# Key blocks on partitions 0 to 95, no zero rows in the value buffers, and an order of tasks from fixed ranks

## The chip, the cores and the metric

The kernel runs on one core of a Trainium2 chip. The core has five engines with instruction streams of their own: TensorE (PE in the profile, with its weight loads as PEld), VectorE (DVE), ScalarE (ACT), GpSimd (POOL) and SyncE (SP), and DMA queues that the engines issue to. The metric is the device time of one execution in microseconds (us). The time before is the median of three runs, 277.43 us (277.42 to 278.05). Every duration below is from one profiled execution, whose span is 275.7 us (275.66 from the first to the last instruction).

## The reference, cut to what matters

B = 4 batches, H = 8 heads, S = 768 positions, D = 64 per head. Attention in chunks of 32 queries over 8 memory keys and a window of 16 keys to the left and 8 to the right; then a Fourier mix over positions and the 512 model channels, a layer norm, and an MLP of 512 to 2048 to 512 with both residuals.

```python
for c in range(S // 32):
    l_start, r_end = max(0, 32 * c - 16), min(S, 32 * c + 32 + 8)
    k_full = np.concatenate([mem_k, k[:, :, l_start:r_end]], axis=2)
    v_full = np.concatenate([mem_v, v[:, :, l_start:r_end]], axis=2)
    a = softmax(q[:, :, 32 * c:32 * c + 32] @ k_full^T / sqrt(D))
    out[:, :, 32 * c:32 * c + 32] = a @ v_full
...
x = out.transpose(0, 2, 1, 3).reshape(B, S, H * D)
mixed = np.real(np.fft.fft(np.fft.fft(x, axis=1), axis=2))
u = x + mixed
un = (u - mean(u)) / np.sqrt(var(u) + 1e-06)
result = u + np.maximum(un @ w_ch1, 0.0) @ w_ch2
```

## The kernel before

**Attention.** There are 16 steps n, each one pair of heads of one batch. q and k are brought in by POOL's DMA queue (`e_load_qk`, L381), turned by TensorE (`e_turn_q`, `e_turn_k`, L409) and copied out of its banks (qT on ScalarE, L427; kTb by L452; the memory keys' columns by L440). v is brought in by SP (`e_load_v`) into one of four buffers `va`, [128, 2, 12, 66] in float32. A tile of such a buffer belongs to 64 queries and has one key per partition: 8 memory keys, 16 of left context, 64 own and 8 of right context, 96 in all. `MEM0` is the partition of the first one, 32 before the change, so the keys stand on partitions 32 to 127; partitions 0 to 31 of `va` are filled with zeros by four copies on ScalarE (`e_low_rows`, L363), and the matching columns of the two `kTb` buffers by a memset. Column D of `va` holds ones, so the value product also gives the softmax's sum. Small memsets and selects (`e_edges` L347 to 349, `e_edge_ones` L354 to 359, `e_masks` L333 to 339) take out keys past the ends.

For each step and each half g of its 12 tiles: 12 score matmuls (`e_scores`, L465), two exponentials (`e_exp`, L475), 24 value matmuls (`e_values`, L517) and the division (`e_norm`, L527 and L528). There is one bank set for scores. Steps 6 to 11 take the form of `a_scores` (L488, L500), and there the PE task `values(n)` of steps 4 to 9 also issues the turns of step n + 2.

**Fourier.** Tables of sines are made at the start: POOL's `e_iota` (L327), angles on VectorE (L342 to L1050), ScalarE's sine for table S (L1188, L1189) and for table D (L1191, L1192), then negatives on VectorE (L1196 to L1202). A one-element activation loads ScalarE's sine functions (L993), another (L1209) its exponential. The first batch (`first_fourier`) folds (L659, L670), splits each value into a high and a low float16 (`hi` on ScalarE, `lo` on VectorE L715), multiplies by the S table (`g_row` L735, `g_rows` L748) and then by the D table (`e_columns`, L759). Batches 1 to 3 do likewise (L549 to L606, rows at L589), the last two with `h_columns` (L780) and `h_mix` (L800, L801); sums with x are at L808 on VectorE or L820 on POOL. Layer norm: statistics on VectorE (`e_stats`, L832 and L833), scale factors on POOL (`e_scale`, L858 to L861), the scaling on ScalarE (L846).

**MLP.** Each batch is three thirds j of 256 rows. The first layer is eight tasks of eight matmuls (`e_ch1`, L897) with a relu on ScalarE (L906). The second layer is plain for batch 0 and (1, 0) (`e_ch2`, L915). For the other eight thirds it is done in seven products of half size: sums of relu blocks on VectorE (`e_s`, L952, in two groups: hidden blocks 0 to 5 and 6 to 7, and one sum more of all eight), products on TensorE (`e_prod`, L964; in the order m1, m2 on the first six blocks, m1, m2 on the last two, m5, m6, m3, m7, m4), and adds to the residual on VectorE (`e_add`, L969) that free the product's bank.

**The order.** Nothing above is emitted in the order of the source. Each piece is a task of class `Plan` with an engine, a cost in us, the tasks it comes after, the buffers it takes and gives back, and a rank. `order()` goes through time, and on each engine starts the task of lowest rank that is ready by its model; the result is the order of instructions on each engine, and the semaphores between engines follow from the data. Where TensorE has nothing near the start, `order()` puts in an idle matmul (`e_fill`, L1024; 20 of them). `shortest(24, 1.5)` calls `order()` 24 times, with normal draws of spread 1.5 added to the ranks, and takes the order that ends first by the model. The tasks' ranks otherwise are the numbers in the `add` calls or the place in the source.

## Time and profile before

| | us |
|---|---|
| median of three runs | 277.43 (277.42 to 278.05) |
| profiled execution, span | 275.66 |
| time outside that span, up to the median | 1.77 |
| TensorE busy | 258.7 (94%) |
| VectorE busy | 204.9 (74%) |
| ScalarE busy | 160.6 (58%) |
| POOL busy | 78.5 (28%) |

The profile's page gives the busy time of each engine, then the span in 40 slices with the busy share in tenths (a 9 is 90% or more), then the chain of work that ended last. A line of the chain has a start, a length, an engine, the operation and the tile, and the line of the kernel. The timeline lists instructions or runs of like instructions: start, length from the first start to the last end, engine, line, operation, out<-in, shape and count, and in brackets the idle time before and what ended it. A window line has the stretch, its length, and then the busy time and number of instructions of PE, PEld, DVE, ACT and POOL, the granted clock, the DMA share and GB/s.

### The profile page before, as it was taken

Reading aid. Unit: us, or ns where it says so; the run is one execution under the profiler, and the core shown is the slowest. Engines: PE = TensorE matmul, PEld = TensorE weight load, DVE = VectorE, ACT = ScalarE, POOL = GpSimd, SP = SyncE. Lnnn points to the kernel's source line nnn. Section 1 sums busy time; section 2 is a strip of 40 time slices with the busy share of each in tenths; the row PEclk is TensorE's granted clock in tenths of the full one; section 3 lists DMA queues with packets and bytes.
Section 4 is the critical chain, followed back from the end, with each engine's and each line's share of the span. In section 5 each row is a group of like instructions: output and inputs, shape, how many; then the busy total and the mean of one; then the engine's idle time right before and its main releaser. Section 6 shows DMA issues by size and latency. Waiting matters only on the chain.

```text
span 275.7 us, 8160 instructions
## 1 busy us (share of the span) xinstructions
PE 258.7 (94%) x3365; PEld 209.8 (76%) x3365; DVE 204.9 (74%) x460; ACT 160.6 (58%) x300; POOL 78.5 (28%) x146
## 2 busy tenths in 40 slices
PE   0489999999999999999999989999999998999995
PEld 0367797888756788658669868888889887888884
DVE  7978999840337999998995997839997996354444
ACT  6888647888555688277646627555373483615150
POOL 8852652350111054045046246001100371000000
PEclk9999999999999999999999999999999999999999
DMA  6999999999997979958989964644960424313152
GB/s 104 203 176 176 193 211 205 198 195 200 174 190 176 204 170 175 212 79 160 241 144 199 183 118 117 123 117 146 132 182 1 95 62 83 111 40 76 64 90 76
DMA packets 116118, 39.98 MB, mean 145 GB/s; under 512 B 104561, under 2 KB 111473, under 8 KB 116081
## 3 DMA queue, kind: packets, MB, share of 16 engines
q1 hardware_dynamic: 93888, 23.54, 47.4%
q0 software_dynamic: 21472, 15.21, 34.8%
q10 hardware_dynamic: 720, 0.72, 0.8%
q8 instruction: 26, 0.43, 0.7%
q14 instruction: 12, 0.09, 0.1%
HBM read 37.36 MB, written 13.37 MB: 184 GB/s over the span
## 4 chain that ended last, share of the span: by engine, by line
PE 80%; DVE 11%; POOL 4%; ACT 2%; issue 1%; POOLq 0%; DVEq 0%
PE ph L897 26%; PE pc L964 14%; PE pc L915 10%; PE ps L589 6%; PE xa L517 5%; PE xo L517 4%; PE pm L759 3%; PE ps L748 3%; DVE S L952 2%; PE sc L465 2%; DVE st L832 2%; DVE xsb L969 2%; PE trk L409 2%; PE idle L1024 1%; PE trq L409 1%; DVE hT L952 1%
## 5 line engine op out<-in xcount | busy, mean ns | idle before, releaser
L897 PE MATMUL ph<-unT,w_sb 128*128 128x256 f16 x768 | 89.6, 273 | 0.0
L897 PEld LDWEIGHTS <-w_sb 128*128 128x128 f16 x768 | 73.7, 98 | 9.3 <-issue 0.3
L906 ACT ACTIVATE hT<-ph 128x512 f16<-128x512 f32 x96 | 56.3, 600 | 39.9 <-PE ph L897 21.1
L964 PEld LDWEIGHTS <-hT 128*128 128x128 f16 x320 | 30.8, 98 | 7.1 <-issue 2.0
L964 PE MATMUL pc<-w_sb,hT 128*128 128x256 f16 x256 | 32.1, 273 | 1.3 <-DVE xsb L969 0.9
L969 DVE TENSOR_TENSOR xsb<-pc,xsb 128x256 f32<-128x256 f32 x57 | 23.7, 420 | 12.6 <-PE pc L964 10.8
L915 PE MATMUL pc<-w_sb,hT 128*128 128x512 f16 x128 | 29.8, 380 | 0.0
L500 ACT ACTIVATE e<-sc,mbias 128x192 f32<-128x192 f32 (+1 forms) x48 | 19.2, 489 | 8.8 <-PE sc L488 8.8
L915 PEld LDWEIGHTS <-hT 128*128 128x128 f16 x128 | 11.8, 98 | 12.9 <-issue 0.4
L952 DVE TENSOR_TENSOR S<-hT 128x768 f16<-128x768 f16 (+1 forms) x16 | 8.5, 533 | 16.1 <-ACT hT L906 15.7
L475 ACT ACTIVATE e<-sc,mbias 128x384 f32<-128x384 f32 x32 | 17.0, 575 | 4.6 <-PE sc L465 4.3
L846 ACT ACTIVATE un<-xsb,rs 128x512 f16<-128x512 f32 x16 | 12.4, 810 | 9.8 <-POOL rs L861 9.8
L964 PE MATMUL pc<-w_t,S 128*128 128x256 f16 x128 | 16.0, 273 | 1.3 <-DVE xsb L969 1.1
L832 DVE BATCH_NORM_STATS2 st<-xsb 128x6 f32<-128x512 f32 x24 | 16.3, 680 | 0.3
L820 POOL TENSOR_TENSOR xsb<-mix,xr 128x512 f32<-128x512 f32 x6 | 8.7, 1459 | 26.6 <-ACT mix L814 26.6
L517 PEld LDWEIGHTS xa<-va,e 128*64 128x64 f32 x384 | 12.9, 142 | 3.8 <-issue 2.7
L601 ACT CAST up<-ps 128x386 f16<-128x386 f32 x16 | 9.7, 606 | 10.4 <-PE ps L589 9.4
L964 PEld LDWEIGHTS <-S 128*128 128x128 f16 x128 | 12.3, 98 | 3.7 <-issue 1.6
L517 PE MATMUL xa<-va,e 128*64 128x65 f32 x384 | 15.2, 230 | 0.0
L517 PE MATMUL xo<-va,e 128*64 128x65 f32 x384 | 14.1, 223 | 0.0
L574 ACT CAST hi<-ff 128x768 f16<-128x768 f32 x12 | 9.7, 829 | 6.3 <-DVE ff L566 6.1
L517 PEld LDWEIGHTS xo<-va,e 128*64 128x64 f32 x384 | 12.6, 138 | 0.5 <-ACT ff L683 0.3
(189 smaller groups left out, 471.9 us busy)
## 6 DMA issues: line engine op xcount, KB each, us to landing
va<-in_v_dram SPq DMA_DIRECT2D x32, 220.0 KB
w_sb<-in_moe_w_ch_dram POOLq DMA_DIRECT2D x8, 512.0 KB, 15.7
out_dram<-xsb SPq DMA_DIRECT2D x12, 256.0 KB
qs<-in_q_dram POOLq DMA_DIRECT2D x12, 192.0 KB, 6.4
ks<-in_k_dram POOLq DMA_DIRECT2D x12, 192.0 KB, 6.9
x_rows<-xsb POOLq DMA_DIRECT2D x3, 768.0 KB, 4.5
xr<-x_back POOLq DMA_DIRECT2D x3, 768.0 KB, 6.0
out_rows<-xsb SPq DMA_DIRECT2D x9, 256.0 KB
```

The source lines that it names most:

```text
L475: nc.scalar.activation(e1[:, :, :, ts(half, 32)], sc[:, :, 0:6, ts(half, 32)], AFT.Exp, bias=mbias[:, half:half + 1], scale=1.0 / math.sqr ...
L500: nc.scalar.activation(to, src, AFT.Exp, bias=mbias[:, half:half + 1], scale=1.0 / math.sqrt(D))
L517: nc.tensor.matmul(xa[64 * half:64 * half + 64, st, hh, 0:65], e1[:, hh, t6, :], v1[:, hh, 6 * g + t6, 0:65], start=True, stop=True)
L589: nc.tensor.matmul(out_[:, sp, :], part[:, ab, sp * 3 + st, c0:c1], tab[:, sp, st, :], start=(st == 0 and i == 0), stop=(st == 2 and i == 1))
L832: nc.vector.bn_stats(st6, xs[b][:, kt, :])
L846: nc.scalar.activation(un, xs[b][:, kt, :], AFT.Identity, bias=rs[:, 1:2], scale=rs[:, 0:1])
L897: nc.tensor.matmul(ph[:, k, :], w1_sb[:, dt, ts(HH * k + i, P)], unT_of[b, j][:, dt, :], start=(dt == 0), stop=(dt == NDT - 1))
L906: nc.scalar.activation(hT_of[b, j][:, :, i, :], ph, AFT.Relu, bias=0.0, scale=1.0 if (b, j) in FAST else -1.0)
L915: nc.tensor.matmul(pc_of[b, j, r], hT_of[b, j][:, k, i, ts(r, P)], w2_sb[:, HH * k + i, :], start=(i + k == 0), stop=(i + k == HH))
L952: nc.vector.tensor_tensor(out_[:, lo:hi], a[:, lo:hi], c[:, lo:hi], op)
L964: nc.tensor.matmul(pc_of[key], a[:, i, :], w[:, i, :], start=(i == 0 and new), stop=(i == HH - 1), skip_group_check=not new)
L969: nc.vector.tensor_tensor(u, pc, u, ALU.add)
```

## The change

The first key goes from partition 32 to partition 0 (`MEM0 = 0`), and `KEYS` = 96 is the number of partitions that are used. The masks and edges move along; `kTb` is set to zero in columns 96 to 127 instead of 0 to 31; the exponential writes 96 partitions instead of 128; a value product contracts over 96 rows instead of 128. The zero fill of `va` and its four tasks go.

`shortest` is replaced by `settled`, which gives 92 tasks (by their number) a fixed rank and calls `order()` once. Tasks in `after` that were not there before are added at several places (folds and splits of the first batch, rows, columns, sums, products, stores); they order tasks in the plan and emit nothing. The order of instructions of every engine changes with this. As built, these moves bear on the text below:

- ScalarE: the two zero copies ahead of the sines and the two among the exponentials are gone. The first exponential stands ahead of the D sines, and the program has four function-table loads on ScalarE, where it had two: for the S sines, the first exponential, the D sines, the next exponential.
- POOL: `e_iota` stands behind the q and k loads of steps 0 and 1 and one `kTb` memset; it was first. VectorE takes the memory keys' casts ahead of the angles, and the first kT copy (L452) ahead of the last two folds of the D angles.
- SP: the v load of step 1 is first and that of step 0 second; the loads from step 6 on, the output stores and the flips change places.
- TensorE: 18 idle matmuls instead of 20; turns and scores of steps 4 and 5 go ahead of some of the first batch's rows and columns; `h_columns(2, 2)`, `rows` of batch 3 and `h_columns(3, 2)` stand between m6 and m3 of the thirds (1, 1), (2, 0) and (2, 2).
- VectorE: in those thirds the statistics or the fold, which stood ahead of sums or adds, come behind them; POOL's L820 tasks move with the new order of the sums, and one of them, with tasks of scale factors, stands at the sums of the third (1, 2).

```diff
 BIGM = 800.0
-MEM0 = 32
+MEM0 = 0
 OWN = MEM0 + NMEM + LEFT
+KEYS = OWN + 2 * CHUNK + RIGHT
...
 
-    def shortest(self, tries, spread):
-
...
-            placed = self.order()
-            if found is None or self.end < found[0]:
-                found = (self.end, i)
-        return placed
+    def settled(self, moved):
+
+        for no, rank in moved.items():
+            self.tasks[no]["rank"] = rank
+        return self.order()
...
         nc.gpsimd.memset(mbias, 0.0)
-        nc.gpsimd.memset(mbias[96:128, 0:1], NEG)
+        nc.gpsimd.memset(mbias[64:96, 0:1], NEG)
         nc.gpsimd.affine_select(out=mbias[:, 1:2], in_=mbias[:, 1:2], compare_op=ALU.is_ge,
                                 fill=NEG, base=-(OWN - LEFT + CHUNK), pattern=[[0, 1]],
                                 channel_multiplier=1)
-        nc.gpsimd.memset(mbias[0:MEM0, 1:2], 0.0)
...
         eng.memset(v1[:, :, :, D:D + 1], 1.0)
-        eng.memset(v1[32:64, :, 0, 0:D], 0.0)
-        eng.memset(v1[96:128, :, NT - 1, 0:D], 0.0)
+        eng.memset(v1[0:32, :, 0, 0:D], 0.0)
+        eng.memset(v1[64:96, :, NT - 1, 0:D], 0.0)
 
     def e_edge_ones(i):
         v1 = va[i]
-        lo, hi = v1[32:64, :, 0, D:D + 1], v1[96:128, :, NT - 1, D:D + 1]
-        nc.gpsimd.affine_select(out=lo, in_=lo, compare_op=ALU.is_ge, fill=0.0, base=32 - OWN,
+        lo, hi = v1[0:32, :, 0, D:D + 1], v1[64:96, :, NT - 1, D:D + 1]
+        nc.gpsimd.affine_select(out=lo, in_=lo, compare_op=ALU.is_ge, fill=0.0, base=-OWN,
                                 pattern=[[0, 2], [0, 1]], channel_multiplier=1)
         nc.gpsimd.affine_select(out=hi, in_=hi, compare_op=ALU.is_ge, fill=0.0,
-                                base=OWN + 63 - 96, pattern=[[0, 2], [0, 1]],
+                                base=OWN + 63 - 64, pattern=[[0, 2], [0, 1]],
                                 channel_multiplier=-1)
         nc.gpsimd.memset(v1[MEM0:MEM0 + NMEM, :, 0, D:D + 1], 1.0)
-
-    def e_low_rows(i):
-        low = va[i][0:MEM0].rearrange("p h t c -> p (h t c)")
-        nc.scalar.copy(low, zero[0:MEM0].to_broadcast([MEM0, 2 * NT * 66]))
...
         for half in halves:
-            nc.scalar.activation(e1[:, :, :, ts(half, 32)], sc[:, :, 0:6, ts(half, 32)],
-                                 AFT.Exp, bias=mbias[:, half:half + 1],
+            nc.scalar.activation(e1[0:KEYS, :, :, ts(half, 32)], sc[0:KEYS, :, 0:6, ts(half, 32)],
+                                 AFT.Exp, bias=mbias[0:KEYS, half:half + 1],
...
         for half in range(2) if g else (part,):
-            to, src = (e1[:, part, :, ts(half, 32)], more[part][:, 0:6, ts(half, 32)]) if g else (
-                e1[:, :, :, ts(half, 32)], sc[:, :, 0:6, ts(half, 32)])
-            nc.scalar.activation(to, src, AFT.Exp, bias=mbias[:, half:half + 1],
+            to, src = (e1[0:KEYS, part, :, ts(half, 32)], more[part][0:KEYS, 0:6, ts(half, 32)]) if g else (
+                e1[0:KEYS, :, :, ts(half, 32)], sc[0:KEYS, :, 0:6, ts(half, 32)])
+            nc.scalar.activation(to, src, AFT.Exp, bias=mbias[0:KEYS, half:half + 1],
...
                     nc.tensor.matmul(xa[64 * half:64 * half + 64, st, hh, 0:65],
-                                     e1[:, hh, t6, :], v1[:, hh, 6 * g + t6, 0:65],
+                                     e1[0:KEYS, hh, t6, :], v1[0:KEYS, hh, 6 * g + t6, 0:65],
...
                 rank=14)
-    t_low, LOW = {}, 110
     for i in range(NV):
         e_ = add("DVE" if i < 2 else "POOL", 0.45, lambda i=i: e_edges(i),
                  rank=(-20, -17.3, 17, 17)[i])
         t_ones[i] = add("POOL", 0.7, lambda i=i: e_edge_ones(i), [e_], rank=(-3.5, 2, 17.1, 17.1)[i])
-        t_low[i] = add("ACT", 1.45, lambda i=i: e_low_rows(i), [t_zero, e_],
-                       rank=(0, 1, 2, 3)[i])
...
     SINES = len(plan.tasks)
-    t_kTz = [add("POOL", 0.45, lambda i=i: nc.gpsimd.memset(kTb[i][:, :, 0:MEM0], 0.0), rank=3)
+    t_kTz = [add("POOL", 0.45, lambda i=i: nc.gpsimd.memset(kTb[i][:, :, KEYS:P], 0.0), rank=3)
...
                                     + [x(n + 2) for x in (e_turn_q, e_turn_k) if n + 2 in JOINED],
-                         xs_ + [lv, t_low[n % NV]], take=("xa",), pick=vp, give=("e1", "e1", "va"))
+                         xs_ + [lv], take=("xa",), pick=vp, give=("e1", "e1", "va"))
...
     add("ACT", 1.4, lambda: nc.scalar.activation(warm, zero, AFT.Exp), [t_sines], rank=SINES)
-    for i in range(2, NV):
-        t_low[i]["behind"] = t_exp[i - 2, 1]
-        t_low[i]["rank"] = t_exp[i - 2, 1]["rank"] + 0.1
...
     def first_fourier():
-        t_rest, t_mid, t_row, pre = {}, {}, {}, {}
+        t_rest, t_mid, t_row, t_rows_, pre, seen, t_lo = {}, {}, {}, {}, {}, [], ([], [])
+        both = None
         for g in range(2):
             for par in range(2):
-                zy = add("DVE", 0.5, lambda par=par, g=g: g_zy(par, g),
-                         [t_norm[0, g], t_norm[1, g], t_sines],
+                both = zy = add("DVE", 0.5, lambda par=par, g=g: g_zy(par, g),
+                         [t_norm[0, g], t_norm[1, g], t_sines, both],
                          take=("dn",) if (par, g) == (0, 0) else ())
                 if g == 1:
-                    w_ = add("DVE", 0.52, lambda par=par: g_w(par), [zy, t_norm[3, 1], pre[par, 1, 0]])
+                    w_ = add("DVE", 0.52, lambda par=par: g_w(par), [zy, t_norm[3, 1], pre[par, 0, 0], pre[par, 1, 0], pre[par, 0, 2]])
...
                         ff = add("DVE", 0.55, lambda par=par, ab=ab: g_both(par, ab),
-                                 pre[par, ab, 1][:2], give=("dn",) if (par, ab) == (1, 1) else ())
+                                 pre[par, ab, 1][:2] + (seen + [pre[p, a, 1][2] for p in range(2) for a in range(2)]
+                                                        if (par, ab) == (1, 1) else []),
+                                 give=("dn",) if (par, ab) == (1, 1) else ())
+                        seen.append(ff)
                     if (par, ab, g) == (0, 0, 1):
                         t_mark.append(ff)
                     hi = add("ACT", 0.5, lambda par=par, ab=ab, g=g: g_hi(par, ab, g),
                              [ff] + (pre[par, ab, 1][2:] if g == 1 else [pre[par, ab, 2]]),
                              take=(("hl",), ("hT",))[par] if (ab, g) == (0, 0) else ())
-                    lo = add("DVE", 0.48, lambda par=par, ab=ab, g=g: g_lo(par, ab, g), [hi],
-                             give=("fold",) if end else ())
+                    lo = add("DVE", 0.48, lambda par=par, ab=ab, g=g: g_lo(par, ab, g),
+                             [hi] + (t_lo[par] if end else []), give=("fold",) if end else ())
+                    t_lo[par].append(lo)
                     if (par, ab, g) == (0, 0, 0):
                         plan.filling = (t_sc[0, 0], add("PE", 0.0, lambda: let_go(fill_of[0]), [lo],
                                                         give=("mlp",)))
                     tag = ("acc", "mlp")[par]
                     mid_ = (par, ab) == (0, 1)
                     rw = add("PE", 1.0, lambda par=par, ab=ab, g=g: g_rows(par, ab, g),
-                             [lo, t_neg] + ([t_row[g]] if mid_ else []),
+                             [lo, t_neg, t_rows_.get((par, ab))] + ([t_row[g]] if mid_ else [])
+                             + ([t_rows_[par, 0]] if end else []),
                              take=(tag,) if g == 0 and not mid_ else (),
                              give=(("hl",), ("hT",))[par] if end else ())
+                    t_rows_[par, ab] = rw
...
                          take=("hl",) if ab == 0 else ())
-                lo = add("DVE", 0.96, lambda par=par, ab=ab: e_lo(b, par, ab), [hi],
-                         give=("fold",) if ab == 1 else ())
+                lo = add("DVE", 0.96, lambda par=par, ab=ab: e_lo(b, par, ab),
+                         [hi, lo if ab else None], give=("fold",) if ab == 1 else ())
                 rw = add("PE", 2.2 if par == 0 and ab == 1 else 1.02,
-                         lambda par=par, ab=ab: e_rows(b, par, ab), [lo, t_sines],
+                         lambda par=par, ab=ab: e_rows(b, par, ab), [lo, t_sines, rw if ab else None],
...
             if b >= HALVED:
-                cols[kt] = add("PE", 0.58, lambda: h_columns(b, kt), allr + t_mir_, take=("acc",),
+                cols[kt] = add("PE", 0.58, lambda: h_columns(b, kt), allr + t_mir_ + [cols.get(kt - 1)], take=("acc",),
...
             cols[kt] = add("PE", 0.9, lambda: e_columns(b, kt),
-                           allr + [t_rows] + (list(t_dn.values()) if kt > 2 else []),
+                           allr + [t_rows] + (list(t_dn.values()) if kt > 2 else [])
+                           + (list(cols.values()) if kt in (2, 5) else []),
...
                 su = add("DVE", 0.8, lambda kt=kt: e_sum_back(b, kt - 3),
-                         [cols.get(kt), t_sum[kt - 3], t_xr[b]],
+                         [cols.get(kt), t_sum[kt - 3], t_xr[b], sa],
...
         for lo, hi in ((0, 6), (6, 8)):
-            s1 = s_op(0, lo, hi, [relu[hi - 1]])
-            s2 = s_op(1, lo, hi, [s1])
-            s3 = s_op(2, lo, hi, [s2])
-        prod, read = {}, {}
+            s1 = s_op(0, lo, hi, [relu[hi - 1], s1])
+            s2 = s_op(1, lo, hi, [s1, s2])
+            s3 = s_op(2, lo, hi, [s2, s3])
+        prod, read, sums = {}, {}, []
...
                               rank=RELU(len(plan.tasks)))
+                sums.append(read[m])
                 if very and m in (7, 4) and (m, c) != (7, 0):
-                    add(("SP", "ACT")[c], 0.5, lambda c=c: e_out_half(b, tiles[1], c), [read[m]],
+                    add(("SP", "ACT")[c], 0.5, lambda c=c: e_out_half(b, tiles[1], c), list(sums),
                         moved=0.5)
             if m == 3:
-                store(b, tiles[0], read[m], ())
+                store(b, tiles[0], list(sums), ())
             elif m == 4 and not very:
-                store(b, tiles[1], read[m], ("xsb",) if end_b else ())
+                store(b, tiles[1], list(sums), ("xsb",) if end_b else ())
...
 
+    moved = {
+        8: 319.48, 10: 296.17, 12: 139.46, 14: 312.16, 15: 139.46, 17: 312.16, 20: -434.07, 34: 328.16,
+        37: -179.62, 38: -507.22, 39: -256.6, 41: -274.77, 45: -575.66, 47: -188.53, 54: -510.81,
+        55: -455.53, 56: -140.81, 57: -35.87, 59: -188.53, 65: -418.19, 86: 317.57, 106: 111.37,
+        109: -406.13, 140: -399.69, 149: -399.69, 180: -397.95, 184: 496.04, 194: 501.16, 203: -400.75,
+        208: -462.33, 226: -41.07, 238: 124.07, 244: 71.5, 245: 173.81, 256: -381.86, 258: 41.45,
+        269: 348.1, 271: 297.03, 274: 267.93, 277: -84.02, 295: 224.5, 305: 219.14, 306: 243.36,
+        311: 376.69, 345: 641.93, 347: 599.99, 353: 279.07, 363: 269.44, 367: 293.12, 381: 269.31,
+        382: 224.22, 384: -999268.57, 385: 351.87, 389: 181.53, 395: 338.27, 396: 251.81, 398: -999233.5,
+        406: 267.22, 440: 1000568.82, 449: 1001095.99, 452: 157.22, 461: 1000782.47, 466: 762.46,
+        483: 324.3, 485: 324.31, 486: 404.33, 497: 379.42, 498: 369.18, 513: 640.98, 528: 559.18,
+        532: 332.36, 555: 959.95, 559: 962.68, 578: 1001028.42, 595: 1001253.63, 615: 452.67, 658: 550.26,
+        664: 404.34, 670: 522.31, 692: 559.17, 698: 559.18, 734: 457, 736: 605.87, 738: 590.29,
+        781: 408.45, 801: 288.79, 803: 306.98, 807: 353.17, 814: 760.5, 834: 783.45, 854: 353.97,
+        935: 780.37,
+    }
     with tc.manual_schedule():
-        for t in plan.shortest(24, 1.5):
+        for t in plan.settled(moved):
             t["emit"]()
 
 
```

## The prediction

> **What bounds the kernel now.** First the page's busy times and slices (each slice is 6.9 us):
>
> ```profile
> PE 258.7 (94%) x3365; PEld 209.8 (76%) x3365; DVE 204.9 (74%) x460; ACT 160.6 (58%) x300; POOL 78.5 (28%) x146
> PE   0489999999999999999999989999999998999995
> PE 80%; DVE 11%; POOL 4%; ACT 2%; issue 1%; POOLq 0%; DVEq 0%
> ```
>
> TensorE is the bound: full from the fourth slice on, but for two slices with an 8 (158.5 to 165 us, 227.5 to 234 us). But for two idle matmuls fewer its instructions are the same after the change, so only their waits and order count: those of the first 31 us, and those behind 31 us. TensorE's timeline shows the latter at a product (L964), where eight matmuls take 0.87 us from start to start when nothing waits (163.08 to 163.95):
>
> ```profile
> 158.88 1.15 PE L964 MATMUL pc<-w_t,S 128*128 128x256 f16 x8
> 160.50 1.03 PE L964 MATMUL pc<-w_t,S 128*128 128x256 f16 x8 [0.47 <-DVE xsb L969]
> 161.96 1.03 PE L964 MATMUL pc<-w_sb,hT 128*128 128x256 f16 x8 [0.43 <-DVE xsb L969]
> 163.08 1.03 PE L964 MATMUL pc<-w_t,hT 128*128 128x256 f16 x8
> ...
> 228.17 1.03 PE L964 MATMUL pc<-w_t,S 128*128 128x256 f16 x8 [0.47 <-DVE xsb L969]
> 229.63 1.03 PE L964 MATMUL pc<-w_sb,hT 128*128 128x256 f16 x8 [0.43 <-DVE xsb L969]
> ```
>
> The starts are 1.62, 1.46 and 1.12 us apart at the first site: 4.20 - 3 x 0.87 = 1.59 us lost. At the second (b 2, j 0) they are 1.23, 1.46 and 0.88 (191.26, 192.49, 193.95, 194.83): 0.96 lost. At the third 1.89, 1.46 and 1.12 (226.28 to 230.75) with 0.07 just before: 1.93 lost. Together 4.48. VectorE's timeline names the cause: what is queued ahead of the adds (L969) that free a bank.
>
> ```profile
> 157.77 0.66 DVE L832 BATCH_NORM_STATS2 st<-xsb 128x6 f32<-128x512 f32 x1
> 158.56 1.02 DVE L952 TENSOR_TENSOR S<-hT 128x256 f16<-128x256 f16 x1
> ...
> 225.92 1.33 DVE L952 TENSOR_TENSOR S<-hT 128x256 f16<-128x256 f16 x1
> ```
> ```profile
> 225.54 1.56 POOL L820 TENSOR_TENSOR xsb<-mix,xr 128x512 f32<-128x512 f32 x1
> ```
>
> At the first site two statistics (L832 with L833, 0.82 each) stand before the second group of sums, at the second site a fold (L565/566, 1.0) stands before the adds. At the first and third site a sum also took 1.02 and 1.33 where its like takes 0.29 (190.35), and a POOL L820 ran over each. VectorE has nothing to give there (windows: length, then busy TensorE, weight loads, VectorE):
>
> ```profile
> 152.00:164.00 12.00, 11.02 (x102) 8.87 (x100) 11.60 (x32) 5.86 (x17) 4.77 (x6) 1.00 1.19 152
> 188.00:196.00 8.00, 7.38 (x67) 6.25 (x65) 7.83 (x19) 2.60 (x4) 0.00 (x0) 1.00 0.99 184
> ```
>
> Now the start. From the chain, ScalarE's timeline, POOL's and VectorE's:
>
> ```profile
> 16.43 1.05 ACT e L475 x2
> 17.48 1.38 ACT va L363
> 18.87 0.69 ACT qT L427
> ```
> ```profile
> 11.67 0.71 ACT L1192 ACTIVATE cosD<-tri,hpi_b 128x512 f16<-128x512 f32 x1
> 12.40 1.28 ACT L1209 ACT_TABLE_LOAD   x1
> 13.69 0.20 ACT L1209 ACTIVATE warm<-zero 128x1 f32<-128x1 f32 x1
> ```
> ```profile
> 0.90 0.57 POOL L327 IOTA tri<- 128x512 f32 x1 [0.40 <-POOLq L1576]
> ```
> ```profile
> 11.60 1.25 DVE L452 COPY kTb<-trk 128x1056 bf16<-128x1056 bf16 x1
> ```
>
> A zero copy (L363) lies on the path. VectorE is busy almost without a gap from 0.88 to 12.85, and the first scores (13.00) need the end of its L452.
>
> **The change, part by part.** The sum is made against the profiled 275.66; 1.77 lies outside it (median 277.43).
>
> *Rows.* Value products over 96 rows, exponentials over 96 partitions: 0. Other work hides nothing here; the rows say that width is time and partitions are not (a 1x512 copy on ScalarE takes 0.58, a 128x512 one 0.60). Bounds: 0 either way by these rows. The memset of kTb covers as many columns as before (0.39), one mbias memset (0.09 on POOL) goes.
>
> *Zero copies.* Two (3.54 to 6.43) ran while ScalarE would have waited anyway (its next input came at 7.12): 0. Two (17.37, 21.94) are worth 1.4 each on ScalarE; they enter below.
>
> *Table switches.* The new order puts the exponentials of step 0 ahead of the D sines (L1191/1192), so ScalarE loads Sin, Exp, Sin, Exp: two loads more, 2 x 1.28 = 2.56.
>
> *Angles.* POOL's iota (L327) goes behind four q/k loads (0.89, 0.67, 0.65, 0.63) and a kTb memset (0.39), ending at 4.85 instead of 1.47. VectorE's angle work follows it; the memory-key cast goes ahead of it but waits for a DMA (landing 3.93). I get 1.8 us of VectorE idle, of which two folds of the D angles (0.75, 0.69) go behind L452: that ends at 13.3 instead of 12.85, first scores 13.5, the S sines at 13.2.
>
> *ScalarE from there:* Exp load to 14.5, exp(0,0) 15.55, qT 16.2, Sin load 17.5, D sines 18.75, Exp load 20.05, exp(1,0) 21.1, which was 17.48. There is one score bank, so the next scores, the values and the first norm (17.73 before, 22.9 now) follow. With no zero copies behind it, step 3's last exponential comes at 31.5 for 29.5. VectorE has 12.2 us of work from the first norm to the first lo (L715; norms 8 x 0.74, kT 1.16, the rest folds of 0.5): 35.1 for 32.67. Fourier's rows start at 36.2 for 33.00 and the columns at 45.95 for 42.97; TensorE has done 1.22 of later work by then (turns 0.48 and 0.46, scores 0.28). Net **+1.75**. TensorE's 20 idle matmuls, 0.20 to 0.50 each, are the cover that is used up. Bounds: 0, if they and the waits absorb all; 3.6, the whole delay of exp(1,0), if the dropped copies win nothing back.
>
> *Idle TensorE.* 18.4 to 21.2 it has nothing. The twelve score matmuls took 0.50 at 13.00 and 0.35 at 20.55 at a granted clock of 1.00. If the slow form returns for that block, two value passes (1.37 against 0.92) and a few turns cost up to 0.9; I take 0, since an idle 0.96 (ending 20.55) was followed by the fast form, and keep 0.9.
>
> *V loads.* v0 goes behind v1, which waits for POOL's edges (about 9.2). v loads take 3.4 to 7 us each here, so I put v0 at 19 for 9.96; values(0,0) wants it at 21.95: 0, cover 3.
>
> *Products.* The statistics and the fold go behind the sums and adds, and the L820s go away from sites one and three; between the products m6 and m3 TensorE gets columns (L780) or rows (L589), 0.4 us or more against a wait of 0.59. Where only this hand-over waits (b 1, j 2 and b 3), it costs 1.05, 0.18 over 0.87. I leave 0.18 per site: -4.48 + 0.54 = **-3.94**, and -0.18 for (b 1, j 2), where values now fill it. Bounds: -4.66 and 0, since VectorE's 97% remains.
>
> *Switches.* Each switch from a dense stream to an attention task costs TensorE 0.094; 25 for 29: **-0.38**.
>
> *New waits.* At (b 1, j 2) an L820 and the L858 group now stand beside sums. Bounds 0 and 1.04 (1.33 - 0.29); I take the middle, **+0.5**.
>
> *The new orderings among tasks* emit no instruction and free no buffer: 0, except through the order counted here.
>
> *Other moves on SP and POOL* (out rows, flips, q and k loads): 0 while each lands ahead of its use; nearest is q6/k6, used at 53 and landing near 52.4 by my count, so a later queue costs one for one.
>
> Sum: 275.66 + 1.75 - 3.94 - 0.18 - 0.38 + 0.5 = 273.4; with 1.77, **275.2**.
>
> **Rivals.**
>
> A, the sum: 275.2, own range 274.0 to 276.8. Chance 0.40.
>
> B, the start is absorbed (20 fills, ScalarE with 13.3 of 17 us busy from 14 to 31): 275.2 - 1.75 = 273.4. Against it: exp(1,0) and the norms are a chain. 0.15.
>
> C, each switch costs its load again before the next activation: 2.56 more, 277.8. [...] Against it: the load at 12.40 begins 0.02 after the cosine ends, and the next activation starts at its end. 0.08. [...]
>
> D, the slower side: the product waits come back. VectorE at 97% must run the statistics somewhere; if they then delay the next adds or scale factors, the 3.94 is not gained: 279.1. It decides from 3.1 kept (278.3). For it, 11.60 of 12 busy; against it, other thirds run the same products with 0.18 lost. 0.20.
>
> E, a late load: v0 lands behind 21.95, or q6 behind 53. From 3.1 us late the kernel is slower: 278.3 to 279. For it, DMA share of 1.1 to 1.3 from 9 to 31 us. 0.17.
>
> **Numbers.** 0.3% (0.83 us) is about what a measurement can tell from no change: 276.6 to 278.3. Faster: A 0.38, B 0.15 = 0.53. Same: A 0.02, C 0.06, D 0.03, E 0.04 = 0.15. Slower: C 0.02, D 0.17, E 0.13 = 0.32. Range: from B with the hand-overs gone too, 273.4 - 0.54 - 0.4 = 272.5, to D, 279.1.
>
> **What would show it.** Four table loads and exp(1,0) ending near 21; rows (L748) starting near 36, columns near 46. At the three sites starts 0.87 to 1.05 apart, statistics behind the adds. It is wrong if columns begin before 45 or after 48, if a product site still loses over 0.5, or if TensorE shows a wait of over 1 us between 46 and 270 that before lacks.

## The result, and the profile after

The changed kernel takes 286.19 us in the median of four runs (285.35 to 286.55) against 277.43: a ratio of 1.0297, 95% interval 1.0272 to 1.0323. The forecast was 275.2 us with a range of 272.5 to 279.1; the kernel became 8.8 us slower. The profiled execution took 285.35 us with a span of 283.6, 8.0 more than the span before. Medians and ranges below are of all executions, while the ratios leave out the three that lay more than 1.5% above the fastest of their kernel (286.96, 284.33 and 669.93 us).

The page of the changed kernel (lines of the code are 18 to 21 lower than before: L897 is now L879, L964 L946, L969 L951, L475 L457, L517 L499, L832 L814):

```profile
PE 260.3 (92%) x3363; PEld 214.1 (75%) x3363; DVE 204.5 (72%) x460; ACT 156.0 (55%) x298; POOL 80.1 (28%) x145
PE   0368999999999999999399999999999999999995
PEclk9999999999999999999899999999999999999999
PE 82%; DVE 10%; POOL 3%; ACT 2%; issue 1%; POOLq 0%; DVEq 0%; ACTq 0%
```

The two slices with an 8 behind the middle are gone. In their place the second slice has a 3 for a 4 and the third a 6 for an 8, and one slice in the middle, which was full, has a 3; behind it the row of the granted clock (PEclk, in tenths), 9 throughout before, has an 8. TensorE's timeline gives the account. The first columns start at 51.20 for 42.97, 8.23 later, with 1.22 of later work done by then: the start lost **7.0**. At the third (1, 0) the first-layer tasks 5, 6 and 7 take 5.68, 1.66 and 1.71 from start to start for 0.87: **6.4** lost. From the columns to the start of the last product but one TensorE took 227.35 for 227.60; with the 1.22 done early and the 6.4 lost, the rest gained 0.25 - 1.22 + 6.42 = **5.45**. The sum, 7.0 + 6.4 - 5.45, is the 8.0.

The gain first. TensorE at the first product site, where 1.59 were lost:

```profile
169.83 1.91 PE L946 MATMUL pc<-w_t,S 128*128 128x256 f16 x16
171.57 0.38 PE L762 MATMUL pm<-sinD,up 128*128 128x256 f16 x2
...
172.13 1.04 PE L946 MATMUL pc<-w_sb,hT 128*128 128x256 f16 x8
173.10 1.03 PE L946 MATMUL pc<-w_t,hT 128*128 128x256 f16 x8
```

m5 and m6 are one dense run of 16 (1.74 from start to start for two), the columns L762 follow, and nothing waits. The sites at (2, 0) and (2, 2) lose 0 and 0.2.

The loss in the middle: chain of work that ended last, from 128 to 145 us (start, length, what):

```profile
130.23 0.96 DVE pq L538
131.19 0.87 DVE pq L539
132.06 0.67 DVE xsb L904
...
132.81 0.99 POOL rstd L861
...
133.86 1.94 POOL rstd L862
...
135.89 0.66 POOL rs L840
...
137.98 0.81 ACT un L828
138.79 0.49 ACT hT L888
...
139.32 4.45 PE ph L879 x24
```

POOL has the MLP's scale factors of batch 1 (`e_rstd`, L861 and L862) ahead of the norm's scale factors of its last two tiles (L840 to L843); it was the other way round. L861 writes the buffer that VectorE's L904 still reads for batch 0, and L904 stands behind folds of batch 2. ScalarE's queue has the scaling L828 ahead of the relus, so the relus wait, and TensorE for a bank.

Only 4.8 of the 6.4 are this wait. Tasks 6 and 7, at 1.66 and 1.71 us, wait for nothing: TensorE came out of the gap with its clock halved. Its timeline, and a window behind the gap:

```profile
130.14 4.54 PE L879 MATMUL ph<-unT,w_sb 128*128 128x256 f16 x40
139.32 4.45 PE L879 MATMUL ph<-unT,w_sb 128*128 128x256 f16 x24 [4.64 <-ACT hT L888]
```
```profile
140.00:142.00 2.00, 2.00 (x11) 1.43 (x10) 0.30 (x1) 2.00 (x4) 0.00 (x0) 0.50 1.09 291
```

Forty of these matmuls took 4.54 us ahead of the gap, 24 took 4.45 behind it, with TensorE busy for 2.00 of 2.00 us at a granted clock of 0.50.

The start: ScalarE's timeline, then TensorE's, then two lines of TensorE's in the kernel before.

```profile
14.57 1.28 ACT L457 ACT_TABLE_LOAD   x1 [0.70 <-PE sc L447]
15.86 1.04 ACT L457 ACTIVATE e<-sc,mbias 96x384 f32<-96x384 f32 x2
16.80 0.79 ACT L409 COPY qT<-trq 128x768 bf16<-128x768 bf16 x1
17.61 1.28 ACT L1170 ACT_TABLE_LOAD   x1
...
20.15 1.28 ACT L457 ACT_TABLE_LOAD   x1
21.45 1.04 ACT L457 ACTIVATE e<-sc,mbias 96x384 f32<-96x384 f32 x2
```
```profile
22.54 0.51 PE L447 MATMUL sc<-qT,kTb 64*128 64x64 bf16 x12 [2.97 <-DVE kTb L434]
...
23.65 1.53 PE L499 MATMUL xa<-va,e 96*64 96x65 f32 x24
...
26.90 1.51 PE L499 MATMUL xa<-va,e 96*64 96x65 f32 x24
...
31.18 0.92 PE L499 MATMUL xo<-va,e 96*64 96x65 f32 x24
```
```profile
16.32 1.37 PE L517 MATMUL xa<-va,e 128*64 128x65 f32 x24
...
18.27 0.88 PE L517 MATMUL xo<-va,e 128*64 128x65 f32 x24
```

Two readings. The loads are there, but the first does not begin when the sines end (13.86): it waits for the scores, since it was put right ahead of the exponential. And TensorE's value products take 1.5 until 28 us and 0.92 from 31 us, where before the fast form was reached at the second value pass (0.88 at 18.27). The twelve score matmuls turn from 0.50 to 0.35 at 17.62 before and at 30.90 here. So for some 13 us more, gaps included, TensorE ran at half its matmul rate (four idle matmuls took 1.46 us at 14.41, three 0.66 at 33.93: 0.32 and 0.16 us apart).

### The profile page after: what moved, and what is told of

Its sections match the earlier page's. It is cut to its first block, busy times and chain, and to the rows that moved or that the text cites. A ratio compares the mean times of both kernels' runs of the same rounds, so it can differ in the third digit from the quotient of the medians.

```text
span 283.6 us, 8124 instructions
## 1 busy us (share of the span) xinstructions
PE 260.3 (92%) x3363; PEld 214.1 (75%) x3363; DVE 204.5 (72%) x460; ACT 156.0 (55%) x298; POOL 80.1 (28%) x145
## 4 chain that ended last, share of the span: by engine, by line
PE 82%; DVE 10%; POOL 3%; ACT 2%; issue 1%; POOLq 0%; DVEq 0%; ACTq 0%
PE ph L879 28%; PE pc L946 16%; PE pc L897 8%; PE ps L571 5%; PE xa L499 5%; PE xo L499 4%; PE ps L730 3%; PE pm L741 3%; PE sc L447 2%; PE trk L391 2%; PE trq L391 1%; PE sc L470 1%; DVE kTb L434 1%; DVE st L814 1%; PE pm L762 1%
## 5 line engine op out<-in xcount | busy, mean ns | idle before, releaser
L879 PE MATMUL ph<-unT,w_sb 128*128 128x256 f16 x768 | 90.7, 276 | 4.6 <-ACT hT L888 4.6
L879 PEld LDWEIGHTS <-w_sb 128*128 128x128 f16 x768 | 74.7, 99 | 15.3 <-issue 5.2
L946 PEld LDWEIGHTS <-hT 128*128 128x128 f16 x320 | 30.9, 98 | 4.5 <-issue 0.8
L946 PE MATMUL pc<-w_sb,hT 128*128 128x256 f16 x256 | 32.0, 273 | 0.1
L951 DVE TENSOR_TENSOR xsb<-pc,xsb 128x256 f32<-128x256 f32 x57 | 23.6, 419 | 10.4 <-PE pc L946 8.9
L897 PE MATMUL pc<-w_sb,hT 128*128 128x512 f16 x128 | 29.3, 380 | 0.0
L897 PEld LDWEIGHTS <-hT 128*128 128x128 f16 x128 | 11.8, 98 | 13.4 <-DVE xsb L510 0.2
L457 ACT ACTIVATE e<-sc,mbias 96x384 f32<-96x384 f32 x32 | 17.1, 576 | 6.3 <-PE sc L447 5.6
L482 ACT ACTIVATE e<-sc,mbias 96x192 f32<-96x192 f32 (+1 forms) x48 | 18.5, 471 | 2.6 <-PE sc L470 2.6
L828 ACT ACTIVATE un<-xsb,rs 128x512 f16<-128x512 f32 x16 | 12.4, 808 | 10.5 <-POOL rs L843 10.2
L814 DVE BATCH_NORM_STATS2 st<-xsb 128x6 f32<-128x512 f32 x24 | 16.4, 685 | 2.2 <-POOL xsb L802 1.9
L934 DVE TENSOR_TENSOR S<-hT 128x768 f16<-128x768 f16 (+1 forms) x16 | 6.8, 423 | 14.4 <-ACT hT L888 13.8
L499 PE MATMUL xa<-va,e 96*64 96x65 f32 x384 | 15.9, 237 | 0.0
L561 DVE TENSOR_TENSOR lo<-ff,hi 128x768 f16<-128x768 f32 x12 | 11.3, 951 | 6.3 <-ACT hi L556 6.3
L499 PEld LDWEIGHTS xa<-va,e 96*64 96x64 f32 x384 | 13.8, 149 | 2.5 <-issue 1.9
L946 PE MATMUL pc<-w_t,S 128*128 128x256 f16 x128 | 15.6, 273 | 0.0
L409 ACT COPY qT<-trq 128x768 bf16<-128x768 bf16 x12 | 9.6, 798 | 10.7 <-PE trq L391 10.7
L499 PE MATMUL xo<-va,e 96*64 96x65 f32 x384 | 14.8, 229 | 0.0
L946 PEld LDWEIGHTS <-S 128*128 128x128 f16 x128 | 12.4, 98 | 1.7 <-issue 0.2
```

The lines of the kernel that those rows point to most:

```text
L457: nc.scalar.activation(e1[0:KEYS, :, :, ts(half, 32)], sc[0:KEYS, :, 0:6, ts(half, 32)], AFT.Exp, bias=mbias[0:KEYS, half:half + 1], scale ...
L482: nc.scalar.activation(to, src, AFT.Exp, bias=mbias[0:KEYS, half:half + 1], scale=1.0 / math.sqrt(D))
L499: nc.tensor.matmul(xa[64 * half:64 * half + 64, st, hh, 0:65], e1[0:KEYS, hh, t6, :], v1[0:KEYS, hh, 6 * g + t6, 0:65], start=True, stop=True)
L561: nc.vector.tensor_tensor(lo[:, ab].rearrange(fl), ff_of[b, par][:, ab].rearrange(fl), hi[:, ab].rearrange(fl), ALU.subtract)
L814: nc.vector.bn_stats(st6, xs[b][:, kt, :])
L828: nc.scalar.activation(un, xs[b][:, kt, :], AFT.Identity, bias=rs[:, 1:2], scale=rs[:, 0:1])
```

## The experiments

Tasks are named by their numbers in the changed plan where a run moves them; `for no, of in [(a, b)]` takes task a out of the placed list and puts it right ahead of b, after which the list is emitted.

### The stall in batch 1

**Scale factors ahead.** 345 is `e_scale` of tiles 2 and 5, 350 `e_rstd`, both of batch 1.

```diff
-        for t in plan.settled(moved):
+        placed = plan.settled(moved)
+        for no, of in [(345, 350)]:
+            ...
+        for t in placed:
```

> The changed kernel with one POOL task moved: the scale factors of batch 1's last two tiles (L840 to L843) go ahead of the MLP's scale factors of batch 1 (L861, L862). Theory: TensorE's stall at the third (1, 0), 4.80 us at its fifth first-layer task and then 0.79 and 0.83 at the two next, is this order: L861 waits until VectorE has read the older scale factors for the last time (L904, to 132.7) because both share a buffer, and L840, ScalarE's scaling and the relus stand behind it. Then the stall goes whole: 6.4 us, 286.2 to about 279.8. Rival: the statistics or VectorE's queue make the scaling late anyhow; then under 2 us are won (284 to 286).

284.16 us (282.39 to 286.96), ratio to before 1.0192 (1.0135 to 1.0249). TensorE's stall at (1, 0) is gone whole: its eight first-layer tasks run in 7.16. So the order was the cause of that stall. But only 2 of the 6.4 were won, since 4.9 come back at the third (1, 1), of which 1.5 is again half clock behind the gap (0.50 from 158 to 160 us, mean of the run 0.994). TensorE, and SP's queue ahead of it:

```profile
157.06 3.25 PE L879 MATMUL ph<-unT,w_sb 128*128 128x256 f16 x15 [2.40 <-DMA unT<-un]
```
```profile
134.50 0.59 SPq L609 DMA_DIRECT2D x_back<-x_rows  x1
135.15 4.35 SPq L610 DMA_DIRECT2D x_back<-x_rows  x1
139.56 1.05 SPq L960 DMA_DIRECT2D out_dram<-xsb  x2
140.70 0.65 SPq L376 DMA_DIRECT2D va<-in_v_dram  x1
...
144.70 5.11 SPq L852 DMA_TRANSPOSE unT<-un  x2
```

The transposes of the last two tiles, which the third (1, 1) needs, were issued at 144.7 although their input was ready at 133.9. Neither forecast of this run held.

**A buffer of its own.** The same order, but L861 writes a buffer that nobody reads (room for it came from three small start-up tiles put into one).

```diff
-        rstd_of[b] = rstd = fpool.tile([P, NST], FP32, tag="rs", bufs=2, name="rstd")
+        rstd_of[b] = rstd = fpool.tile([P, NST], FP32, tag="rstd", bufs=2, name="rstd")
```

> The changed kernel with the order as it is and two buffers for the MLP's scale factors alone, so that L861 doesn't wait for L904. Theory: L861 starts with the last statistics, about 127.9 for 132.8, and only its own 2.9 us still stand ahead of L840; scaling ends near 134.5 for 138.0 and the stall shrinks to 0.5 to 2 us: 281 to 282.5. If it were not the shared buffer that holds L861, nothing changes (286).

283.68 us in one run. No stall is left at (1, 0) here either, so it was the shared buffer that held L861, and L861's own 2.9 us are covered. The loss at (1, 1) is 4.5 us, close to that of the run above; the forecast of 281 to 282.5 missed for that reason.

**Transposes ahead too.** 347 and 349 are the transposes, 408 the load back of batch 2's mirrored rows, 704 a relu that follows the scaling.

```diff
+        for no, of in [(345, 350), (347, 408), (349, 704), (408, 704)]:
```

> As the run with the scale factors moved, and on SP the two transposes of batch 1's last tiles (L852) go ahead of the load back of batch 2's mirrored rows (L609, L610), the stores and the v loads of steps 14 and 15. Theory: with the first stall gone, TensorE waits at the third (1, 1) for these transposes (2.48, 0.79, 0.67 and 1.00 us there: 4.9), since SP issues them at 144.7 behind 10 us of transfers; ahead of those they land by 142 and the wait goes: 284.2 - 4.9 = 279.3. Rival: what is put behind them (x_back, v14, v15) is late then and TensorE waits for that: 281 to 284.

285.04 us (282.08 to 285.38), 1.0241 (1.0187 to 1.0295): no gain on the run with the scale factors alone. TensorE no longer waits for the transposes, but loses 4.46 + 1.16 + 0.41 us at the same place, the first to the next transfer and the other two to the half clock behind that gap (0.50 from 158 to 160 us, mean of the run 0.993; value passes of 1.48 and 1.56 for 0.92 and 0.87). VectorE:

```profile
156.24 0.56 DVE L510 TENSOR_TENSOR xsb<-xa,zs 128x384 f32<-128x384 f32 x1 [5.04 <-DMA va<-in_v_dram]
```

This division writes the first tile of batch 3 into the buffer that the store of batch 0's last tile (L960, issued at 148.37 behind a v load) still reads; the profile puts the wait down to another DMA of the same queue. That it is the store is shown by two runs below that differ in its place alone: all three repairs (282.34 us), and the same with this store ahead (276.25 us).

### The start

**Two loads less.** 32 and 33 are the last folds of the D angles, 45 the first kT copy, 105 the D sines, 106 the one-element exponential, 47 the first exponential.

```diff
+        for no, of in [(32, 45), (33, 45), (105, 47), (106, 47)]:
```

> The changed kernel with the D sines and the one-element exponential ahead of the first exponential, and VectorE's D angles ahead of the first kT copy: two table loads less, everything else as it is. Theory (the start is ScalarE's chain of loads): step 0's second exponential ends near 19.1 for 22.5, the columns start near 47.5 for 51.2, 282 to 283. Rival (the start is TensorE at half its matmul rate until 30 us): the second exponential ends earlier but the values still take 1.4 each, and less than half of the 3.4 reaches the columns: 284 to 285.5.

283.71 us in one run. The second exponential ends at 19.2 (19.1 was expected), 3.3 earlier, but the columns start at 49.56, 1.6 earlier: TensorE's values still take 1.5 until 26 us. So both causes are at work, and the loads are the smaller at the columns.

**Idle matmuls in the gaps.**

```diff
+        for behind, count in [(58, 8), (76, 9)]:
+            at = [t.get("no") for t in placed].index(behind) + 1
+            placed[at:at] = [idle] * count
```

> The changed kernel with idle matmuls put into two of TensorE's gaps: eight behind the second step's q turn (11 to 14 us) and nine behind the third step's k turn (19.5 to 22.5 us); the chain on ScalarE stays. Theory (TensorE has fallen back to half its matmul rate in these gaps: the values from 23.65 to 28.3 take 1.35 to 1.46 where later ones take 0.75 to 0.85): they take 0.85 from the start, the first norms come 1 to 2 us earlier, the columns 1.5 to 3 us: 283 to 284.7. Rival (the rate has nothing to do with the gaps, or ScalarE's chain sets all): 286, or up to 1 us more.

282.63 us in one run; the columns start at 48.27, 2.9 earlier. TensorE's timeline:

```profile
17.01 0.50 PE L447 MATMUL sc<-qT,kTb 64*128 64x64 bf16 x12 [1.72 <-ACT e L457]
...
19.57 2.00 PE L1003 MATMUL idle<-dz 128*128 128x384 bf16 x9
22.59 0.35 PE L447 MATMUL sc<-qT,kTb 64*128 64x64 bf16 x12 [1.02 <-ACT e L457]
...
23.25 0.88 PE L499 MATMUL xa<-va,e 96*64 96x65 f32 x24
```

With ScalarE's chain as it was, the first value pass takes 0.88 for 1.53. So about 2.9 of the 7.0 are half rate. The eight first idle matmuls raised the rate too (0.35 at 14.18), and the slow form is back at 17.01 behind an idle 1.72, with a granted clock of 0.50 from 17 to 20 us (mean of the run 0.986).

**The start's order of the kernel before.** A list of 164 task numbers and idle matmuls, in the order in which the kernel before emits them up to the first rows, goes ahead; the rest follows in the changed order.

```diff
+        START = [18, 3, 2, 0, 9, 19, 1, 11, 38, ..., 135, 125]
+        rest = [t for t in placed if "no" in t and t["no"] not in START]
+        for t in head + rest:
```

> The changed kernel with the order of the kernel before for everything up to the first Fourier rows (20 idle matmuls and two table loads as there, the zero copies gone), and the changed order from there on; both stalls of batch 1 stay possible. Theory (the start alone lost 7.0: columns at 51.20 for 42.97, 1.22 of that work done early): columns start between 43 and 45 with the later work done, 279 to 280. Rival: loads on SP and POOL in their new places hold the columns back or the stall at (1, 0) grows: over 281.

282.25 us (280.28 and 284.21), 1.0164 (1.0078 to 1.0250): columns at 48.67 and not near 44. With two loads, the iota first and the first scores at 13 us as before, TensorE was still slow: the value passes of the next run, which starts in the same order with the same rows, take 1.53 to 1.57 until 27 us. The order was not the cause of that.

**The new rows alone.** The kernel before with the change's rows and masks; the zero copies emit nothing.

> The kernel before with the new rows alone: keys on partitions 0 to 95, exponentials and value products over 96, the four zero copies emit nothing; the order of everything else is that of the kernel before. Theory: rows cost and win nothing, two of the four copies were on the chain (1.38 and about 0.6), and part of it is eaten by idle matmuls: 275.4 to 277.2. Rival: only TensorE's later stretch counts and the start's waits absorb it: 277.4 within 0.3%. If 96 rows made the products slower or faster, each of the 768 value matmuls would show it (0.217 to 0.23 us).

281.11 us (278.40 to 281.74, ten runs), 1.0103 (1.0075 to 1.0130). Slower by 3.4 than the kernel before beside it, with nothing moved and four copies less: both forecasts missed. The value passes take 1.53 to 1.57 until 27 us, for 0.88 from 18.27 before.

**Copies or rows.** Two runs beside each other: the zero copies put back, onto the unused partitions; and then all 128 rows as well.

```diff
     def e_low_rows(i):
+        low = va[i][KEYS:P].rearrange("p h t c -> p (h t c)")
+        nc.scalar.copy(low, zero[KEYS:P].to_broadcast([P - KEYS, 2 * NT * 66]))
...
-                                     e1[0:KEYS, hh, t6, :], v1[0:KEYS, hh, 6 * g + t6, 0:65],
+                                     e1[:, hh, t6, :], v1[:, hh, 6 * g + t6, 0:65],
```

> The kernel with the new rows alone, and the four zero copies of the kernel before put back (onto partitions 96 to 127, which nothing reads): order and instructions of the kernel before, but exponentials and value products over 96 partitions. Question: why TensorE stays at half its matmul rate until 28 us with the new rows and only until 17 us before. Theory rows (a product over 96 rows counts for less in what raises the rate than one over 128): nothing changes, values before 25 us take 1.35 to 1.5, 280 to 281.7. Theory copies (their absence moves the start): values take 0.85 from about 18 us on, 277 to 278.

> As the run with the zero copies put back, and exponentials and value products over all 128 partitions: the kernel before with its keys moved by 32 partitions. Theory rows: the rate rises at about 17 us, 277.4 within 0.5%. If the place of the keys (other DMA destinations) is the cause, it stays at 280 to 281.5.

With 96 rows 281.11 us (278.16 to 281.32), with 128 rows 277.90 (277.70 to 278.56), ratio to before 0.9994 (0.9981 to 1.0007). It is the rows. The same window of both (busy TensorE with its matmuls first), 96 rows and then 128:

```profile
16.00:28.00 12.00, 12.00 (x208) 9.42 (x206) 6.73 (x14) 8.67 (x12) 2.44 (x6) 1.00 0.93 168
```
```profile
16.00:28.00 12.00, 10.86 (x274) 8.76 (x269) 8.79 (x20) 10.50 (x16) 3.27 (x7) 1.00 1.00 169
```

TensorE with 96 rows is busy all of the 12 us, issues 208 matmuls and stays slow; with 128 rows it issues 274 in 10.86 us. The row's clock says 1.00 in both. And the timelines from the first value pass:

```profile
16.28 1.57 PE L517 MATMUL xa<-va,e 96*64 96x65 f32 x24
...
18.89 1.53 PE L517 MATMUL xo<-va,e 96*64 96x65 f32 x24
...
24.54 1.57 PE L517 MATMUL xo<-va,e 96*64 96x65 f32 x24
```
```profile
16.21 1.57 PE L517 MATMUL xa<-va,e 128*64 128x65 f32 x24
...
18.64 0.88 PE L517 MATMUL xo<-va,e 128*64 128x65 f32 x24
```

Here one pass of 128 rows and the rate is up; four of 96 and it is not. The exponentials change their partitions with the products in this pair (1.04 and 1.05 for two); that the products and not they matter is argued, from the matmuls being what changes speed. With 96 rows seven of the ten executions took 280.4 to 281.3 us and three 278.2 to 278.6, as long as those with 128. That the rate rose earlier in these three is likely but not shown, since only a slow one was profiled.

**Idle matmuls at the very start**, with the new rows alone and with the kernel before:

```diff
+        for behind, count in [(23, 28), (48, 6)]:
```

The 28 follow the first idle matmul; task 48 is a k turn of the start, behind which the second run has 4 in place of 6.

> The kernel with the new rows alone and 34 idle matmuls more, 28 at the very start, where TensorE has nothing before 8.7 us, and 6 behind the first k turn. Theory (half the rate is what the new rows lost): TensorE is at its full rate from about 6 us on, the first values take 0.85, and the 3.4 us come back with some of the half rate that the kernel before has until 17 us: 276.0 to 277.6. Rival (the loss is elsewhere): 280 to 281.7.

> The kernel before with 32 idle matmuls more at the same two places. Theory: its first scores, turns and values (0.50, 0.88 and 1.37 at half rate) shorten to 0.35, 0.54 and 0.92, but VectorE's and ScalarE's chains hold most of it: 276.4 to 277.4. Rival: it stays within 0.3%.

281.68 us, 1.0134 (1.0095 to 1.0172), and 277.84, 0.9996 (0.9979 to 1.0014): no gain. With the new rows TensorE was at its full rate by 8.8 us (0.53 for a turn) and lost it again about 15.6 us, behind gaps of 0.48, 1.07 and 0.87 (scores of 0.35 at 12.89 and 0.50 at 15.59); the 96-row passes then, at 1.53 to 1.57, did not bring it back before 29 us (granted clock 0.50 from 16 to 26, mean of the run 0.974). In the kernel before it was lost about 13.3 us, behind gaps of 0.69 and 1.18 (0.35 at 13.00, 0.50 at 15.87), and back by 20.7 (0.35). The early rise was held in neither run, and won nothing.

### What the change is worth without its losses

**The start, the scale factors and the transposes together.**

> The changed kernel with all three repairs: the start's order of the kernel before, the scale factors ahead, the transposes ahead. Theory: what is left of the change is the gain at the product sites and the switches, 5.4 us by TensorE's account from the columns on, and the zero copies: 272 to 273. Rival: earlier work meets the transfers' own times, and a new wait for a DMA gives part of it back: 274 to 277.

282.34 us, 1.0132 (1.0049 to 1.0215). Columns at 46.66; 6.5 us went at (1, 1) to the store of batch 0's last tile, 3.9 in waiting and 2.6 at the half clock behind it (value passes of 1.57 and 1.54 for 0.92 and 0.87, mean clock of the run 0.988).

**The product sites alone.** The kernel before up to the first-layer tasks of (1, 1), then the remaining tasks in the changed order (a task whose set of banks has none free takes one of the other set).

```diff
+        for t in placed[:at] + [task[no] for no in REST]:
```

> The kernel before (keys on partitions 32 to 127, zero copies, its own order) up to the first-layer tasks of the third (1, 1); from there the order of the changed kernel for all that is left. So the reordered product sites alone. Theory: the waits at the three sites and at m6 go as they did in the changed kernel, where TensorE loses 0.1 to 0.25 us there instead of 4.48: 277.4 - 4.0 = 273.4, 272.8 to 274. Rival: the gain in the changed kernel came only because everything on SP and POOL was late there, and here TensorE meets a wait for a DMA or a statistic in its place: 275 to 277.5.

275.17 us (274.91 to 275.58), 0.9906 (0.9885 to 0.9928). The three sites wait no more, but of the 4.0 expected 2.5 came: a new 1.27 us at rows of batch 2 (143.96) and 0.49 at (2, 2). Between the theory and the rival.

**128 rows in the changed order.**

> The changed kernel with exponentials and value products over all 128 partitions and zero copies of rows 96 to 127, all four at 3.5 to 9.5 us, where ScalarE waits; its order as it is. Theory: what the 96 rows cost is the half rate of TensorE until 30 us, but its gaps (11 to 14, 15.7 to 17, 19.6 to 22.5 us) also hold the rate down, so the full rate comes with the first value products, some 4 us behind 22.5: 283 to 285 for 286.2. If the gaps alone held it: 286.

285.10 us (284.70 to 286.20), 1.0269 (1.0238 to 1.0299): 1.1 less in the median, with an interval that overlaps that of the changed kernel. The columns start at 50.63 for 51.20. Behind a gap of 2.97 us the three first value passes take 1.46, 1.36 and 1.44, as they do with 96 rows; the fast form comes with the scores at 28.52. So here the gaps hold the rate down as well.

**All repairs.** 128 rows with zero copies, the start's order, scale factors and transposes ahead, and the store of batch 0's last tile (698) ahead of the v loads.

```diff
+        for no, of in ((345, 350), (347, 408), (349, 704), (698, 704), (408, 704)):
```

> The changed kernel with 128 rows and zero copies, the start's order of the kernel before, the scale factors and the last transposes of batch 1 ahead, and the store of batch 0's last tile ahead of the v loads of steps 15 and 14 (the wait that took the place of the others: a division's write to the buffer that this store reads). Theory: start as before (columns near 44.2 with 1.22 of later work done, 43.0 without), no stall in batch 1, product sites as in the changed kernel: 272 to 273.5. Rival: yet another late transfer at the third (1, 1): 275 to 279.

> The repaired kernel (start's order of the kernel before, batch 1's scale factors, transposes and last store ahead) with 96 rows and no zero copies, as the change has it. Theory: the 96 rows hold TensorE at half its matmul rate until 24 to 30 us here too, which costs 3 to 4 us, less about 1 for the two zero copies on the chain: 275 to 277.5 for 273.1. If the rows cost only in company of the changed start's gaps: 272 to 273.5.

> The repaired kernel with 128 rows, and the zero rows of the last two value buffers set by POOL (idle from 17 to 25 us) instead of ScalarE. Theory: the two copies are on ScalarE's chain of exponentials (17.40 to 18.9 and 22.36 to 23.9); without them the first rows start 0.5 to 1.5 us earlier: 271.6 to 272.6. Rival: idle matmuls and the V loads fill the gap: 273.1 within 0.3%.

Repaired: 273.06 us (272.71 to 273.39), 0.9833 (0.9808 to 0.9858). TensorE waits nowhere over 0.3 us behind the columns, and its granted clock stays at 1.00, so the chain of late transfers ended with that store. The same with 96 rows and no zero copies: 276.25 us (274.44 to 276.61), 0.9923 (0.9888 to 0.9958), columns at 48.35 for 45.05; the rows cost about 3 us here too. The repaired kernel with two of the zero fills on POOL: 272.56 us (272.37 to 272.75), 0.9797 (0.9764 to 0.9830), the fastest of all, though its interval overlaps that of the repaired kernel: columns at 44.96 for 45.05, so the copies were hardly on the path. Its page:

```profile
PE 256.5 (95%) x3365; PEld 211.3 (78%) x3365; DVE 202.9 (75%) x460; ACT 156.6 (58%) x298; POOL 81.4 (30%) x147
PE   0499899999999999999999999999999999999995
```

## Why the prediction was wrong

*Rows, 0 with bounds of 0 either way.* This failed. The price was looked for in the duration of one instruction, which did not change; it lies in the rate of all matmuls around it, 3.2 us in the median by the pair above. The row that spoke for a price was in the prediction: the same twelve matmuls at 0.50 and 0.35. It was used for gaps alone. That the rate is what the rows moved is shown; what raises it is not.

*Idle TensorE, 0 with 0.9 kept.* Mis-sized: holding the rate up in the gaps was worth 2.9 in the changed order. This and the rows overlap: either keeps the rate down. Of the 7.0 at the start, two loads less gave back 1.6, idle matmuls 2.9 and 128 rows alone 0.6; 128 rows with the start's order as before gave 6.15 (columns at 45.05). What the last 0.9 is stays open.

*Table switches and ScalarE's chain.* 1.28 a load was right, four loads were there, and nothing waits after a load (a switch at 14.57, the exponential at 15.86; 17.61 and 18.90; 20.15 and 21.45). So rival C fell. The end of step 0's second exponential was put at 21.1 and came at 22.5: the S sines end at 13.86 for 13.2, and the first load waits another 0.7 with the exponential for the scores, where the prediction let it begin with the end of the sines. The columns came at 51.2 for 45.95 forecast, past the bound of 48 that the text set itself.

*V loads, 0 with cover.* Right: the first value pass, at 23.65, waits for no load.

*Products, switches, m6.* Right in mechanism and too small in size: 4.0 after the charge for new waits, 5.45 measured in the changed kernel. The feared meeting of L820 with the sums at (1, 2) cost nothing there. By itself, in the order of the kernel before, the reordering gave 2.5, since waits for other work came up behind it.

*Other moves on SP and POOL, 0.* This is the second step that failed, with 6.4 us in the changed kernel, 4.8 of it a wait and 1.6 the half clock behind it, and three waits behind each other: scale factors behind a buffer's last reader, transposes behind ten us of transfers, a store behind a v load. Rival E had a late transfer as its mechanism but named v0 and q6; the moves in batch 1 were not costed one by one, though each was in the list of orders. Each hid the next: taking away the first won 2.0, the first two 1.15, all three with the start and the rows 13.1. The wait of 4.64 us at (1, 0) is also the sign of being wrong that the prediction named, a wait of over 1 us between 46 and 270.

Two readings in the prediction are loose, and neither carries the sum: the 128x512 operation of 0.60 us is a relu and no copy, and the DMA share from 14 to 17 us is 0.92, below the 1.1 to 1.3 given for rival E.

## What to carry to other kernels

A change of shape that left the time of its own instructions alone (the first value pass 1.57 with 96 rows and with 128, two exponentials 1.04 and 1.05) still cost 3.2 us here, by the rate of the matmuls around it (the same twelve scores 0.50 at 21.10 and 0.35 at 20.83): compare a known group of matmuls in both kernels, not the changed instruction alone. When an order changes, go through each engine's queue for what now stands behind a late reader of a reused buffer, stores included; and when a stall is taken away and little is won, look at the same place for the next transfer in the queue. The stall at (1, 0) cost TensorE more than its 4.64 us, with 1.6 at a granted clock of 0.50 behind it; count both. The table load right ahead of the first exponential waited 0.70 us for that exponential's scores; at a one-element activation ahead of it, in the run with two loads less, the load began when the cosine ended (15.16), before the scores started (15.64).

## What the runs showed of the hardware

- Busy time alone did not tell TensorE's rate. With 96-row value passes it was busy for 12 of 12 us (16 to 28) at half rate (passes of 1.53 to 1.57); with 128 rows in the same place the fast form was there after one pass (1.57 at 16.21, 0.88 at 18.64), and around nine idle matmuls of 128x384 at 19.57 us of the changed order the twelve scores went from 0.50 at 17.01 to 0.35 at 22.59. One pass is no rule: in the changed order three passes of 128 rows stayed slow (1.46, 1.36 and 1.44) behind a gap of 2.97 us. What raises the rate is not shown.
- Gaps at the thirds (1, 0) and (1, 1) of 4.64, 2.40, 4.30 and 3.73 us (the changed kernel, scale factors ahead, transposes ahead, three repairs) were each followed by a granted clock of 0.50, which cost 1.6, 1.5, 1.6 and 2.6 us more. A gap of 1.10 us, in the run of the product sites alone, was not: its clock stays at 1.00 (mean of the run 1.000). The spread of the executions goes with this: with the scale factors ahead 282.39 us came with a mean granted clock of 1.000, 283.89 and 284.42 with 0.994, 286.96 with 0.988.
- In the start, the rate was down behind shorter gaps too: with idle matmuls in the gaps the scores took 0.35 at 14.18, and behind an idle 1.72 us 0.50 at 17.01, with a clock of 0.50 from 17 to 20 us.
- The granted clock in the profile's rows reads 1.00 throughout the slow start of the changed kernel (8 to 30 us, value passes of 1.51 to 1.57), ahead of the first rise, and 0.50 in the stretches given above, where the rate fell after one. So in these runs 0.50 was a sign that the rate was down, but 1.00 near the start was none that it was up; the duration of a known group of matmuls was (twelve scores 0.50 or 0.35).
